# Cross-attention and maxout layers on one core: PSUM pools regrouped, three weight products run as one group, a subtraction moved to GpSimd

## The chip, the cores and the metric

The kernel runs on one core of one Trainium2 chip. Times are device microseconds (us) of whole executions; each number given for a kernel is the median of several, with the lowest and highest. One execution of each kernel was also profiled, and the times inside a kernel are read from that trace. The span in a profile is some 1.8 us shorter than the time of the same execution. PE is TensorE, DVE is VectorE, ACT is ScalarE, POOL is GpSimd, SPq is the queue of the engine that issues transfers.

## The reference, cut to what matters

```python
# attention between x (8 batches, 8 heads, 512 tokens, 64) and a state of 32 rows per head
a  = softmax(scale * x @ state.T)      # 512 x 32 per head
xread = a @ state
a2 = softmax(scale * state @ x.T)
sread = a2 @ x
t  = concat([xread, sread])            # per batch 544 rows of 512
# maxout layer on all 4352 rows
out = maximum(t @ w1, t @ w2) @ w_out  # w1, w2: 512 x 1024; w_out: 1024 x 512
```

The kernel uses max(h1, h2) = max(h1 - h2, 0) + h2. With Wc = [W1 - W2, W2 Wout], 512 x 1536, and a the attention weights, it forms S Wc once per batch (S is the state, so this is small), then a (S Wc): the first 1024 columns go through a relu and Wout, the other 512 are added to the output. So each batch needs: scores, exp, normalisation, `a` transposed into `aT`, S Wc in three chunks of 512 columns, a first layer (aT times S Wc, 16 matmuls of 512 columns), and four output chunks of 10 matmuls each.

## The kernel before

PSUM is used as two pools of four banks, one for the output chunks (`acc`), one for everything else (`ps`):

```python
psum = ctx.enter_context(tc.tile_pool(name="ps", bufs=4, space=bass.MemoryType.PSUM))
accs = ctx.enter_context(tc.tile_pool(name="acc", bufs=4, space=bass.MemoryType.PSUM))
```

A chunk of S Wc takes two banks, eight matmuls of 64x32 tiles, and two copies out. For the batches below TWO the first two chunks are computed as S W1 - S W2, in two terms, since W1 - W2 (`wcat`) isn't there yet:

```python
def u_sw(b, ch, engs="VA"):
    pg = [bank(), bank()]
    two = b < TWO and ch < 2               # TWO = 3
    terms = ((sbd, w1b), (sneg, w2b)) if two else ((sbd, wcat),)
    ...                                    # 8 matmuls per term
    for g in range(2):
        copy(engs[g], SW[b][:, g, ch * 512:(ch + 1) * 512], pg[g])
```

The attention of batch n = b + 1 is woven between the output chunks of batch b. Slot 8 stands behind output chunk 0, slot 11 behind chunk 3:

```python
put(8, lambda: u_sc(n, 0), lambda: u_sc(n, 1))          # scores, exp, normalisation
put(8, lambda: compact_x(n + 1, 0), lambda: compact_x(n + 1, 1))
put(9, lambda: u_sw(n, 0))
put(10, lambda: u_sw(n, 1), lambda: u_sr(n))
put(10, lambda: d_at(n))                                # transposing DMA: aT <- a
put(10, lambda: d_xt(n + 1))                            # transposing DMA: xt <- xc, right behind it
put(11, lambda: u_srt(n), lambda: u_sw(n, 2))
```

And in the loop over batches, on VectorE:

```python
if b == 1:
    put_states(rest, sT)                   # copy of the states of batches 3..7 into sbd
    fill[9].append(lambda: w_sub(0))       # W1 - W2, a quarter each, on VectorE
    fill[11].append(lambda: w_sub(1))
if b == 2:
    fill[8].append(lambda: w_sub(2))
    fill[9].append(lambda: w_sub(3))
```

The softmax here doesn't subtract the row's maximum and nothing guards it: scores larger than these inputs give would overflow.

## Time and profile before

| | before |
|---|---|
| time, us | 159.56 (158.77 to 160.09, 3 runs) |
| span of the profiled execution | 158.4 |
| mean granted TensorE clock in it | 0.984 |

The chain of waits is the work that ended last, followed back from the last instruction. I cut it into stages at the start of each batch's first layer and at the scores:

| stage of the chain, us | before |
|---|---|
| 1 until batch 1's first layer begins | 43.90 |
| 2 that layer | 4.41 |
| 3 first layers of batches 2 to 7 | 21.94 |
| 4 from the scores to the next first layer, six times | 53.69 |
| output chunk 0, ahead of the scores, six times | 12.96 |
| 5 from the end of the last first layer to the end | 21.49 |
| sum | 158.39 |

### The profile page before, as it was taken

The page shows a single profiled execution, that of the slowest core. Times are in us where ns is not written, and L with a number is a line of the kernel's source. Part 1 is how long each engine was busy: PE and PEld are TensorE (multiplying, and loading weights), DVE is VectorE, ACT ScalarE, POOL GpSimd, SP SyncE. Part 2 cuts the span into 40 slices and gives each one's busy share as a digit, 9 for nine tenths or more (in the row PEclk, how much of TensorE's full clock was granted, in tenths as well). Part 3 has the DMA queues.
Part 4 walks back from the last instruction along what each step waited for, and adds up shares of the span by engine and source line. Part 5 has one row for each costly group of instructions (what it writes and reads, how often), then busy time and mean ns, then how long its engine had stood idle before and what let it go on. Part 6 is the DMA issues. An engine that isn't in the chain of part 4 may idle for free.

```text
span 158.4 us, 3054 instructions
## 1 busy us (share of the span) xinstructions
PE 145.6 (92%) x1272; PEld 67.4 (43%) x1272; DVE 92.2 (58%) x155; ACT 74.5 (47%) x125; POOL 35.1 (22%) x40
## 2 busy tenths in 40 slices
PE   6779699997789999988999999999999999999990
PEld 1356353343435334523453444445444534664430
DVE  5378367946995849595755466555647554731110
ACT  3064357635773828452746447363827234621100
POOL 3015300800740540074005402520500050000000
PEclk9978999999999999999999999999999999999998
DMA  3999999669499299909981997593079033501531
GB/s 92 371 390 389 384 377 290 232 116 227 152 289 291 73 106 326 302 0 105 345 284 25 152 299 256 38 297 132 0 107 342 19 35 82 217 0 37 163 137 66
DMA packets 37789, 29.88 MB, mean 189 GB/s; under 512 B 24848, under 2 KB 33040, under 8 KB 36880
## 3 DMA queue, kind: packets, MB, share of 16 engines
q1 hardware_dynamic: 37776, 29.69, 68.5%
q8 instruction: 10, 0.16, 0.5%
q14 instruction: 3, 0.02, 0.1%
HBM read 15.20 MB, written 8.91 MB: 152 GB/s over the span
## 4 chain that ended last, share of the span: by engine, by line
PE 72%; DVE 10%; DMA 10%; ACT 2%; POOL 2%; issue 1%; SPq 0%; DVEq 0%; POOLq 0%; ACTq 0%
PE acc L315 27%; PE ps L300 16%; PE acc L311 7%; PE acc L387 4%; PE ps L275 4%; DMA xf<-in_x_dram 4%; DMA aT<-a 3%; DMA xt<-xc 3%; PE ps L213 2%; PE ps L342 2%; PE acc L352 2%; POOL a L223 2%; PE ps L376 2%; PE ps L236 1%; DVE es L220 1%; DVE sbd L64 1%
## 5 line engine op out<-in xcount | busy, mean ns | idle before, releaser
L315 PE MATMUL acc<-wo,r 128*128 128x512 bf16 x256 | 60.8, 379 | 0.0
L315 PEld LDWEIGHTS <-r 128*128 128x128 bf16 x256 | 24.7, 98 | 29.9 <-issue 0.8
L300 PE MATMUL ps<-aT,swt 128*128 128x512 bf16 x128 | 29.9, 379 | 0.9 <-DVE r L290 0.4
L223 POOL TENSOR_TENSOR a<-e,er 128x512 bf16<-128x512 bf16 x13 | 14.4, 1124 | 63.0 <-ACT e L216 38.3
L290 DVE TENSOR_SCALAR r<-ps 128x512 bf16<-128x512 f32 x32 | 21.8, 690 | 7.9 <-PE ps L300 7.6
L64 DVE COPY ob<-acc 128x512 f32<-128x512 f32 x16 | 11.0, 686 | 23.0 <-PE acc L315 23.0
L288 ACT ACTIVATE r<-ps 128x512 bf16<-128x512 f32 x32 | 19.3, 602 | 8.9 <-PE ps L300 8.8
L64 DVE CAST swt<-ps 128x512 bf16<-128x512 f32 x24 | 16.4, 685 | 12.0 <-PE ps L275 12.0
L62 ACT CAST swt<-ps 128x512 bf16<-128x512 f32 x24 | 14.3, 595 | 14.0 <-PE ps L275 14.0
L62 ACT COPY ob<-acc 128x512 f32<-128x512 f32 x16 | 9.4, 590 | 21.2 <-PE acc L315 19.9
L300 PEld LDWEIGHTS <-swt 128*128 128x128 bf16 x128 | 11.8, 97 | 16.9 <-issue 2.7
L311 PE MATMUL acc<-swt,aT 128*128 128x512 bf16 x64 | 18.7, 381 | 0.0
L66 POOL CAST xp<-xf 128x2048 bf16<-128x2048 f32 (+1 forms) x8 | 14.1, 1762 | 14.3 <-DMA xf<-in_x_dram 14.3
L216 ACT ACTIVATE e<-ps 128x512 bf16<-128x512 f32 x16 | 8.8, 595 | 14.9 <-PE ps L213 14.9
L62 ACT CAST xc<-xf 128x1024 bf16<-128x1024 f32 x13 | 13.0, 1051 | 0.0
L220 DVE TENSOR_REDUCE es<-e 128x16 f32<-128x512 bf16 x16 | 10.6, 662 | 2.5 <-ACT e L216 2.5
L133 PE MATMUL ps<-warm 128*128 128x512 bf16 x18 | 7.2, 541 | 1.3 <-POOL warm L119 1.3
L275 PE MATMUL ps<-wcat,sbd 64*32 64x512 bf16 x144 | 7.4, 387 | 1.1 <-DVE wcat L361 1.1
L387 PE MATMUL acc<-wo,w2t 128*128 128x512 bf16 x32 | 7.4, 379 | 0.0
L311 PEld LDWEIGHTS <-aT 128*128 128x128 bf16 x64 | 4.9, 97 | 5.4 <-issue 1.8
L275 PEld LDWEIGHTS <-sbd 64*32 64x32 bf16 x192 | 2.7, 89 | 10.4 <-issue 8.4
L213 PE MATMUL ps<-sbd,xt 128*128 128x64 bf16 x128 | 5.4, 196 | 1.5 <-DMA xt<-xc 0.8
(65 smaller groups left out, 109.2 us busy)
## 6 DMA issues: line engine op xcount, KB each, us to landing
xf<-in_x_dram SPq DMA_DIRECT2D x8, 1024.0 KB, 7.7
out_dram<-ob SPq DMA_DIRECT2D x7, 1024.0 KB, 5.1
w2f<-in_moe_w_dram SPq DMA_DIRECT2D x2, 1024.0 KB, 10.1
wof<-in_moe_w_out_dram SPq DMA_DIRECT2D x4, 512.0 KB, 11.4
w1f<-in_moe_w_dram SPq DMA_DIRECT2D x2, 1024.0 KB, 15.3
out_dram<-ob SPq DMA_DIRECT2D x4, 256.0 KB, 2.0
out_dram<-obs SPq DMA_DIRECT2D x8, 64.0 KB, 1.7
s_f<-in_state_dram SPq DMA_DIRECT2D x1, 320.0 KB, 13.8
```

Source lines behind the costliest of these rows:

```text
L62: nc.scalar.copy(o, i)
L64: nc.vector.tensor_copy(o, i)
L66: nc.gpsimd.tensor_copy(o, i)
L220: nc.vector.tensor_reduce(d["es"][:, g], d["e"][:, g].rearrange("p i c n -> p (i c) n"), axis=mybir.AxisListType.X, op=ALU.add)
L223: mul.tensor_mul(d["a"][:, g].rearrange("p c i n -> p i c n"), d["e"][:, g], d["er"][:, g].rearrange("p (i c) -> p i c", i=4).unsqueeze(3) ...
L275: nc.tensor.matmul(pg[g][32 * i:32 * i + 32, :], sneg[gs, b, i, :] if k else sbd[gs, b, 2 * i + g, g, :], w[gs, i, ch * 512:(ch + 1) * 512 ...
L288: nc.scalar.activation(out=o, in_=p, func=ACTF.Relu)
L290: nc.vector.tensor_scalar(o, p, scalar1=0.0, scalar2=None, op0=ALU.max)
L300: nc.tensor.matmul(p, SW[b][:, g, f * 128:(f + 1) * 128], AT[b][:, g, :], start=(g == 0), stop=(g == 1))
L311: nc.tensor.matmul(OB[b][1 + c], AT[b][:, g, c * 128:(c + 1) * 128], SW[b][:, g, FF:WC], start=(g == 0), stop=False)
L315: nc.tensor.matmul(OB[b][1 + c], R[b][:, f, c * 128:(c + 1) * 128], wo[:, f, :], start=False, stop=(f == NF - 1))
L387: nc.tensor.matmul(WO[i], w2t[:, i, f, :], wo[:, f, :], start=(f == 0), stop=(f == NF - 1))
```

## The change

Its intent is to take waits and small costs from around TensorE, which is busy 92% of the time. It has five parts: the start is put in another order (the w2b cast earlier, both halves of x1 on ScalarE, one warm-up of three matmuls fewer); PSUM is one ring of eight banks once batch 1 begins; the three S Wc chunks of a batch run as one group; W1 - W2 goes to GpSimd and is ready before batch 2 (batch 1 uses its first half, in one of its two chunks); the last output chunk is computed and stored in halves. The copy of the late states moves from the beginning to the end of batch 1.

```diff
-    TWO = 3
+    TWO = 2
+    def one_ring():
+        early.close()                     # the two pools of 4
+        pools["ps"] = pools["acc"] = ctx.enter_context(tc.tile_pool(name="ring", bufs=8, ...))
-    def u_sw(b, ch, engs="VA"):
+    def sw_mm(b, ch, engs="VA"):          # matmuls now, copies later
...
-        two = b < TWO and ch < 2
+        two = b < TWO and ch < 2 and (b, ch) != (1, 0)
...
+        return lambda: [copy(engs[g], SW[b][:, g, ch * 512:(ch + 1) * 512], pg[g]) for g in range(2)]
+    def u_sw(b, *chs):
+        for out_of in [sw_mm(b, ch) for ch in chs]:
+            out_of()
...
-            put(9, lambda: u_sw(n, 0))
-            put(10, lambda: u_sw(n, 1), lambda: u_sr(n))
-            put(10, lambda: d_at(n))
+            put(9, lambda: u_sr(n))
+            put(10, lambda: u_sw(n, 0, 1, 2), lambda: d_at(n))
...
-            put(11, lambda: u_srt(n), lambda: u_sw(n, 2))
+            put(11, lambda: u_srt(n))
...
-        nc.vector.tensor_sub(wcat[:, :, cs], w1f[:, :, cs], w2f[:, :, cs])
+        nc.gpsimd.tensor_sub(wcat[:, :, cs], w1f[:, :, cs], w2f[:, :, cs])
...
     w_cast(w1b, w1f, 0)                   # at the start
+    w_sub(0)
+    w_sub(1)
...
         if b == 1:
-            put_states(rest, sT)
-            fill[9].append(lambda: w_sub(0))
-            fill[11].append(lambda: w_sub(1))
-        if b == 2:
-            fill[8].append(lambda: w_sub(2))
-            fill[9].append(lambda: w_sub(3))
+            fill[11].append(lambda: put_states(rest, sT))
```

Cut here: the new order of the start, `l2_end` (two halves of 256 columns, each with its copy and its store, on two queues), and a helper.

More of the change, by code (lines that the diff above doesn't have):

```diff
@@ L49, with bank @@
     big = ctx.enter_context(tc.tile_pool(name="big", bufs=2))
-    psum = ctx.enter_context(tc.tile_pool(name="ps", bufs=4, space=bass.MemoryType.PSUM))
-    accs = ctx.enter_context(tc.tile_pool(name="acc", bufs=4, space=bass.MemoryType.PSUM))
+    early = ctx.enter_context(ExitStack())
+    pools = dict(ps=early.enter_context(tc.tile_pool(name="ps", bufs=4, space=bass.MemoryType.PSUM)),
+                 acc=early.enter_context(tc.tile_pool(name="acc", bufs=4, space=bass.MemoryType.PSUM)))
     ctx.enter_context(tc.manual_schedule())
-    def bank(dtype=F32):
-        return psum.tile([128, 512 if dtype == F32 else 1024], dtype, tag="ps", name="ps")
+    def bank(dtype=F32, kind="ps"):
+        return pools[kind].tile([128, 512 if dtype == F32 else 1024], dtype, tag="b", name=kind)
     def acc():
-        return accs.tile([128, 512], F32, tag="acc", name="acc")
+        return bank(kind="acc")
+    def one_ring():
+        early.close()
+        pools["ps"] = pools["acc"] = ctx.enter_context(tc.tile_pool(name="ring", bufs=8, space=bass.MemoryType.PSUM))
     def copy(eng, o, i):
@@ L68, in negate @@
     def negate(eng, o, i):
-        if eng == "A":
-            nc.scalar.activation(out=o, in_=i, func=ACTF.Copy, scale=-1.0)
-        else:
-            (nc.vector if eng == "V" else nc.gpsimd).tensor_scalar(o, i, scalar1=-1.0, scalar2=None, op0=ALU.mult)
+        (nc.vector if eng == "V" else nc.gpsimd).tensor_scalar(o, i, scalar1=-1.0, scalar2=None, op0=ALU.mult)
     def run(*units):
@@ L170, with new_x @@
     st = {}
+    def new_x(b):
+        if b not in st:
+            st[b] = dict(xt=at.tile([128, 2 * H, 128], BF16, tag="xt", name="xt"))
     def cast_x(b, parts=(("P", slice(0, 8)),)):
-        xp = xio.tile([128, H, NC, 66], BF16, tag="xp", name="xp")
+        new_x(b)
+        xp = st[b]["xp"] = xio.tile([128, H, NC, 66], BF16, tag="xp", name="xp")
         nc.gpsimd.memset(xp[:, :, :, 64:65], 1.0)
@@ L177, in cast_x @@
             copy(e, xp[:, hs, :, 0:64], xf_t[b][:, hs].rearrange("p h (c d) -> p h c d", c=NC))
-        st[b] = dict(xp=xp, xt=at.tile([128, 2 * H, 128], BF16, tag="xt", name="xt"))
     def compact_x(b, g, eng="A"):
+        new_x(b)
         if g == 0:
@@ L278, in u_sw @@
                                      start=(k == 0), stop=(k == len(terms) - 1))
-        for g in range(2):
-            copy(engs[g], SW[b][:, g, ch * 512:(ch + 1) * 512], pg[g])
+        return lambda: [copy(engs[g], SW[b][:, g, ch * 512:(ch + 1) * 512], pg[g]) for g in range(2)]
+    def u_sw(b, *chs):
+        for out_of in [sw_mm(b, ch) for ch in chs]:
+            out_of()
     flip = [0]
@@ L327, in l2 @@
     def l2(b, fill):
-        for c in range(NC):
+        for c in range(NC - (b == B - 1)):
             l2_open(b, c)
@@ L334, in l2, with l2_end @@
             l2_out(b)
+        else:
+            l2_end(b, NC - 1)
+    def l2_end(b, c):
+        ob = OB[b][0]
+        dst = out[b * L:b * L + S].rearrange("(p c) n -> p c n", c=NC)
+        cs = slice(c * 128, (c + 1) * 128)
+        for h in range(2):
+            hs = slice(h * 256, (h + 1) * 256)
+            p = acc()[:, 0:256]
+            mm = [(AT[b][:, g, cs], SW[b][:, g, FF + h * 256:FF + (h + 1) * 256]) for g in range(2)]
+            mm += [(R[b][:, f, cs], wo[:, f, hs]) for f in range(NF)]
+            for k, (w, v) in enumerate(mm):
+                nc.tensor.matmul(p, w, v, start=(k == 0), stop=(k == NF + 1))
+            copy("A" if h else "V", ob[:, c, hs], p)
+            (nc.scalar if h else nc.sync).dma_start(out=dst[:, c:c + 1, hs], in_=ob[:, c:c + 1, hs])
     def moe_sread():
@@ L432 @@
     u_norm(0, 1, nc.vector)
+    negate_states()
     warm_up(3)
-    for i in range(4):
-        w_wo(0, i)
-    for i in range(4):
-        w_wo(1, i)
+    for q in range(2):
+        for i in range(4):
+            w_wo(q, i)
+    w_cast(w2b, w2f, 1)
+    wo_cast(2, "P")
+    w_t(1, 0, "V")
+    w_t(1, 1, "A")
     u_at(0, "V")
     u_srt(0)
-    w_cast(w2b, w2f, 1)
-    negate_states()
-    w_t(1, 0, "V")
-    w_t(1, 1, "A")
-    wo_cast(2, "P")
     wo_cast(3, "V")
-    warm_up(3)
     for i in range(4):
@@ L449 @@
     w_cast(w1b, w1f, 0)
-    w_wo(3, 0)
-    w_wo(3, 1)
+    w_sub(0)
+    w_sub(1)
+    for i in range(4):
+        w_wo(3, i)
     u_sw(0, 0)
-    w_wo(3, 2)
-    w_wo(3, 3)
-    l1(0, {}, range(0, 2))
     u_sw(0, 2)
-    l1(0, {}, range(2, 4))
-    cast_x(1)
+    l1(0, {}, range(0, 4))
     for c in range(NC):
@@ L461 @@
     w_cast(w1b, w1f, 1)
-    compact_x(1, 0, "A")
-    compact_x(1, 1, "V")
+    compact_x(1, 0)
+    compact_x(1, 1)
     d_xt(1)
+    cast_x(1)
+    w_sub(2)
+    w_sub(3)
     cast_states("P", rest)
+    load_x(3)
     sT = d_states(rest)
@@ L474 @@
     cast_x(2)
-    load_x(3)
     l2_add(0, 0, range(4, 8))
@@ L480 @@
     l2_close(0, 1)
+    u_sw(1, 1)
+    u_sr(1)
     compact_x(2, 0)
     compact_x(2, 1)
-    u_sw(1, 1)
-    u_sr(1)
-    u_at(1, "V")
     l2_add(0, 2, range(4, 8))
     l2_close(0, 2)
-    u_sw(1, 2)
-    u_srt(1)
+    u_at(1, "V")
     l2_add(0, 3, range(4, 8))
@@ L492 @@
     d_xt(2)
+    u_sw(1, 2)
+    u_srt(1)
     l2_out(0)
+    one_ring()
     for b in range(1, B):
```

## The prediction

> **What bounds the kernel now.** I read the page's busy shares first, then the chain that ended last, then TensorE's own waits, then the timeline around each wait.
>
> ```profile
> PE 145.6 (92%) x1272; PEld 67.4 (43%) x1272; DVE 92.2 (58%) x155; ACT 74.5 (47%) x125; POOL 35.1 (22%) x40
> ...
> PE 72%; DVE 10%; DMA 10%; ACT 2%; POOL 2%; issue 1%; SPq 0%; DVEq 0%; POOLq 0%; ACTq 0%
> ```
>
> TensorE (PE) is busy 92% of the span and makes 72% of the chain. So a gain must come from fewer matmuls on TensorE or from its few waits. VectorE (DVE) and transfers have 10% of the chain each, some 16 us each. TensorE's waits with a named cause are short:
>
> ```profile
> PE ps L376 <- DVE w2b L64: 1.5, 1, 1.5
> ...
> PE ps L275 <- DVE wcat L361: 1.1, 1, 1.1
> PE ps L254 <- DVE swt L64: 0.9, 1, 0.9
> PE ps L213 <- DMA xt<-xc: 0.8, 1, 0.8
> ...
> PE ps L300 <- DVE r L290: 0.4, 1, 0.4
> PE ps L300 <- DMA aT<-a: 0.3, 1, 0.3
> ```
>
> All of these are waits that the change touches. The chain in order of time shows one steady batch (start us, us, what):
>
> ```profile
> 95.70 0.47 PE ps L213 x16
> 96.17 0.43 PE acc L311 x2
> 96.60 1.73 PE acc L315 x8
> 98.32 0.34 PE ps L275 x8
> 98.66 0.54 PE acc L311 x2
> 99.20 1.73 PE acc L315 x8
> 100.93 0.34 PE ps L275 x8
> 101.27 0.37 PE ps L236 x30
> 101.64 0.54 PE acc L311 x2
> 102.17 1.73 PE acc L315 x8
> 103.90 0.06 PE ps L260
> 103.96 0.34 PE ps L275 x8
> 104.30 3.69 PE ps L300 x16
> ```
>
> TensorE has no hole here: scores (L213), output chunks of 2.16 (L311 and L315), three S Wc chunks (L275) of 0.34 each, then the next batch's first layer (L300) of 3.6 to 3.7. From scores to that layer is 8.60, and a whole batch 14.4. But the attention goes another way at the same time: scores, exp, sums, the product on GpSimd (POOL), a transposing DMA into aT, and only then L300. In batch 2 this is what ended last:
>
> ```profile
> 68.14 1.52 DVE L361 TENSOR_TENSOR wcat<-w1f,w2f 128x1024 bf16<-128x1024 f32 x1
> ...
> 70.59 1.24 SPq L245 DMA_TRANSPOSE aT<-a  x1
> ...
> 71.70 0.41 PE L275 MATMUL ps<-wcat,sbd 64*32 64x512 bf16 x8 [1.09 <-DVE wcat L361]
> ...
> 75.47 2.76 PE L300 MATMUL ps<-aT,swt 128*128 128x512 bf16 x12 [0.33 <-DMA aT<-a]
> ```
>
> The subtraction on VectorE holds TensorE 1.09 us, and aT lands at 75.42, just ahead of L300. The trace's landings of aT, against the start of L300: 59.55 and 59.60, 75.42 and 75.47, 89.86 and 89.93, 104.11 and 104.30, 118.11 and 118.74, 132.30 and 133.18. The first four batches have no slack there; this decides what the regrouping is worth.
>
> [...]
> - [...] this cast takes 0.69 us elsewhere and 1.70 here, ending about 0.55 after GpSimd's does.
>
> ```profile
> 27.96 1.89 POOL L66 CAST xp<-xf 128x2048 bf16<-128x2048 f32 x1 [8.61 <-DMA xf<-in_x_dram]
> ...
> 28.70 1.70 DVE L64 CAST w1b<-w1f 128x1024 bf16<-128x1024 f32 x1
> ```
>
> - [...] No such operation is in this trace; its bf16 product of 512 elements takes 1.05, which scales to 2.1.
> - [...] eight 64x32 matmuls take 0.34, sixteen take 0.56, so eight more cost 0.22 and each entry some 0.12; the 128x128 pair after them takes 0.54 instead of 0.43.
>
> **The change part by part.** Stages are cut by the chain of waits.
>
> 1. Until batch 1's first layer begins (43.90 before). The w2b cast moves ahead of the aT copy on VectorE. Its data landed at 15.72 by the trace, so the transposes (L376) can follow the matmuls that end at 17.95; the 1.5 us hole goes, and so does a warm-up of 0.65. All four w_wo(3) chunks then end near 23.0. Now the w1 columns bound: they land at 22.15, ScalarE's cast takes 1.05, so S W1 starts near 23.3 (24.26 before); the first layer's four pieces must wait for the WO copies and swt copies, near 25.1, and end near 26.9 (28.07 before): 1.2 us earlier. Next the x1 data land at 27.91 whatever I do; both compact halves are now on ScalarE, 2 x 1.05, so the transposing DMA starts near 30.1 (32.13 before[...]), and at 4.4 lands near 34.6. I allow 0.4 for load_x(3), now issued beside it. Scores near 34.9 (36.59 before). Then VectorE's in-order copies, 7.3 us before, set the rest: batch 1 begins near 42.3. Saved 1.6. The subtractions[...] end before the product that needs GpSimd at about 38.5.
> 2. Batch 1's first layer, 43.90 to 48.31, 4.41. VectorE copied sbd from sT in it for 1.93, the four PSUM banks filled and TensorE stopped. That copy goes to the end of batch 1, and the ring has 8 banks. A free run is about 3.65. Saved 0.75. (The copy then delays VectorE's relus in batch 2 by some 1 us; 8 banks take that up.)
> 3. First layers of batches 2 to 7, six times 3.63 to 3.69. With no swt copy in front of the relus and 8 banks I put them at 3.55 (sixteen times 0.216 is 3.46). Saved 0.6.
> 4. From scores to the next first layer, six times: 9.13, 10.09, 8.67, 8.60, 8.60, 8.60. TensorE's own work becomes 0.47 + 3 x 2.16 + 2 x 0.11 + 0.37 + 0.06 + SW (0.12 + 3 x 0.22 = 0.78) = 8.38, 0.22 under the 8.60; the two-term S W of batch 2 falls to the same. But aT doesn't get faster: it landed 9.08, 10.04, 8.60, 8.41, 7.97, 7.72 after the scores. Only the second changes: without the subtraction the aT issue is 4.2 after the scores, as in the others, not 5.2, so 9.0. The later of the two gives 9.1, 9.05, 8.65, 8.45, 8.38, 8.38 = 52.0, against 53.7. Saved 1.7, of which 1.05 is the subtraction and only 0.65 the group.
> 5. The end. The last copy of 512 columns on ScalarE takes 0.59, and its store of 256 KB lands 2.06 later. A half has 256 columns, 0.38 by the rs rows, and 128 KB; the 64 KB stores land in 1.7. Saved 0.2 + 0.2 = 0.4. The halved matmuls cost nothing: N = 256 runs at 0.109 each (32 in 3.49).
>
> Sum 1.6 + 0.75 + 0.6 + 1.7 + 0.4 = 5.05. From 159.56 that is 154.5; I add 0.2 for small frictions of a new order and say **154.7**.
>
> **The rivals.**
> - The regrouping gives its whole 0.22 per batch and aT follows. For: aT lands later where the xt transpose is issued close behind it (4.97 and 4.83) than in batch 6, which has none (3.50), so another order of transfers could speed it. Against: the same two transfers stay in the same order. TensorE's 8.38 six times is 50.3, 1.7 us under my 52.0: 153.0.
> - The subtraction on GpSimd takes the place of VectorE's: [...] cast_states and the product of batch 1 slip. For: both engines are woken by the same landing. Against: at 7.61 VectorE started 0.03 ahead of GpSimd on such a landing. Stage 1 would lose 1.3: 156.0.
> - load_x(3), issued early, slows the xt transpose by more than my 0.4, up to 2 us. For: 1 MB behind it in the same queues. It would cost 1 to 1.5: about 156.
> - Six banks taken at once make TensorE wait for copies. Against: when the group is issued, its banks' last users (two relus, one output chunk, two scores, another chunk) ended over 2 us earlier. It would cost 0.3 a batch, 156.5.
>
> **Range and chances.** The certain parts are the subtraction in batch 2 (1.05), the sbd copy (0.75) and the end (0.4); with those alone it is 157.4. The start is a chain of many orders, and two rivals bear on it. If it gives nothing, 156.3; if all rivals for the better hold, 153. A range of 153.0 to 156.6 should hold 8 of 10. Faster by over 2% means under 156.4: 0.86. Within 2%: 0.13. Slower: 0.01.
>
> **What would show it.** Step 1: scores of batch 1 near 35, the first layer of batch 1 near 42.3, and no wait of L376 for w2b. Step 2: 3.65 for that layer and no wait for a relu. Step 4: in batches 1 to 3 TensorE's wait for aT grows from 0.3 in total to 1.2 to 1.6; no wait for the subtraction; S Wc as one group of 0.78. If that wait stays small, and the interval is 8.4 in batches 1 to 3 too, the first rival is right. VectorE's busy time falls by 5.5[...]. If GpSimd's subtractions take 3 us or more each, or the w1b cast on VectorE is over 2 us, the second rival is right; if the first xt transpose takes over 5.5, the third. Wrong altogether if a wait for PSUM banks appears before L275 in each batch.

## More of the kernel before

The clock is one more thing to look at before two traces are compared. This row of the page gives the granted clock in 40 slices of the span, 9 for full speed. Before:

```profile
PEclk9978999999999999999999999999999999999998
```

There was one dip, in the third and fourth slice; the trace's clock records put it at 10.01 to 13.42 us.

## The result, and the profile after

The changed kernel took 155.44 us at the median of 4 runs (152.12 to 158.12); the kernel before, beside it, 159.6. The ratio of fast runs is 0.9589, with a 95% interval of 0.9476 to 0.9703: faster. A ratio is the mean time of one kernel's fast runs over that of the other's of the same rounds, so not quite the ratio of the medians. Here the difference matters: an execution more than 1.5% above the fastest of its kernel is labelled slow and left out, and the changed kernel spreads over 6 us, so the ratio rests on the two fastest of its four runs. The medians give 155.44 / 159.6 = 0.974.

The spread is itself a finding. The kernel before lies within 158.5 and 160.7 in all its runs here. The changed kernel's ten executions took 152.12, 152.56, 153.81, 154.25, 154.86, 155.56, 155.84, 156.88, 157.06 and 158.12.

The profiled execution took 153.81, with a span of 152.0. The page's busy shares and the chain's shares:

```profile
PE 142.4 (94%) x1255; PEld 68.7 (45%) x1255; DVE 85.5 (56%) x151; ACT 75.4 (50%) x126; POOL 44.4 (29%) x44
...
PE 84%; DVE 7%; DMA 4%; ACT 2%; issue 0%; SPq 0%
```

The chain is now 84% TensorE, from 72%; VectorE's part falls from 10 to 7 and that of transfers from 10 to 4. TensorE does 17 matmuls fewer, VectorE loses 6.7 us, GpSimd gains 9.3. The chain, stage by stage, against the prediction and against the quietest variant (experiment plus16 below):

| stage of the chain, us | before | predicted | changed | plus16 |
|---|---|---|---|---|
| 1 until batch 1's first layer | 43.90 | 42.3 | 43.86 | 42.24 |
| 2 that layer | 4.41 | 3.65 | 3.62 | 3.62 |
| 3 six first layers | 21.94 | 21.3 | 20.70 | 20.70 |
| 4 scores to first layer, six | 53.69 | 52.0 | 50.10 | 50.10 |
| output chunk 0, six | 12.96 | - | 12.96 | 12.96 |
| 5 the end | 21.49 | 21.1 | 20.80 | 20.8 |
| sum | 158.39 | | 152.04 | 150.4 |

So stage 1 gave nothing in this execution, where 1.6 was expected, and stages 3 and 4 gave 4.83, where 2.3 was expected. The sum came out near the number all the same. A steady batch of the changed kernel in the chain (start us, us, what):

```profile
77.56 0.47 PE ps L221 x16
...
80.19 0.37 PE ps L244 x32
80.55 0.54 PE acc L322 x2
...
82.82 0.77 PE ps L283 x24
83.59 0.54 PE acc L322 x2
84.13 1.73 PE acc L326 x8
85.85 0.06 PE ps L268
85.91 3.45 PE ps L311 x16
```

L221 is the scores, L283 the S Wc, L311 the first layer (L213, L275 and L300 before). The group of 24 takes 0.77 where three groups of 8 took 0.34 each. The first layer comes 8.35 after the scores, where it was 8.60, and takes 3.45, where it was 3.69: what stands just in front of it is now an ordinary 128x128 transpose (L268) and no longer a group of 64x32 matmuls. There is no aT anywhere in this chain, and among TensorE's waits none for aT.

**Stage 1.** The clock row of this execution:

```profile
PEclk9965999999999999999999999999999999999999
```

The dip is longer: the records show half the clock for 6.83 us (8.97 to 15.80), where the profile of before has it for 3.41. TensorE came to the first WO matmul at 15.88 instead of 14.33, and everything behind it on VectorE was late too. The timeline of GpSimd and of VectorE (start us, us, engine, line, what):

```profile
21.73 5.41 POOL L389 TENSOR_TENSOR wcat<-w1f,w2f 128x1024 bf16<-128x1024 f32 x2 [2.82 <-DMA w1f<-in_moe_w_dram]
```

```profile
22.08 2.85 DVE L70 CAST w1b<-w1f 128x1024 bf16<-128x1024 f32 x1
```

The w1 columns landed at 21.65. VectorE was still in its w_out cast, GpSimd began 0.35 us ahead of it, and VectorE's w1b cast needed 2.85 us instead of 0.69, ending 0.55 after GpSimd's first subtraction (24.92 and 24.37). That is the prediction's second rival, come true in this execution. The kernel before shows the like twice: casts of the same form that began while GpSimd was in a cast took 1.70 and 1.74 us, and each ended 0.55 after it. What holds VectorE there the traces don't show. It turns on which of the two begins first, so on tenths of a microsecond; the next profile shows the other outcome. Dip and long cast can be told apart by the profile of sub_back below: it has as long a dip (8.41 to 15.24, first WO matmul at 15.73) and no subtraction on GpSimd, its cast took 0.69, and its batch 1 began at 42.72. So most of the 1.4 us between this execution's 43.86 and the next profile's 42.42 goes with the long cast.

### The profile page after: what moved, and what is told of

Same layout as the page of the kernel before. It is cut to its first block, busy times and chain, and to the rows that moved or that the text cites.

```text
span 152.0 us, 3031 instructions
## 1 busy us (share of the span) xinstructions
PE 142.4 (94%) x1255; PEld 68.7 (45%) x1255; DVE 85.5 (56%) x151; ACT 75.4 (50%) x126; POOL 44.4 (29%) x44
## 4 chain that ended last, share of the span: by engine, by line
PE 84%; DVE 7%; DMA 4%; ACT 2%; issue 0%; SPq 0%
PE acc L326 34%; PE ps L311 18%; PE acc L322 10%; DMA xf<-in_x_dram 4%; PE ps L283 3%; PE ps L221 2%; PE ps L370 2%; PE acc L380 2%; PE acc L415 2%; DVE w1b L70 2%; PE ps L244 2%; PE ps L404 2%; PE acc L360 1%; PE ps L203 1%; PE acc L378 1%; PE ps L136 1%
## 5 line engine op out<-in xcount | busy, mean ns | idle before, releaser
L326 PE MATMUL acc<-wo,r 128*128 128x512 bf16 x248 | 58.9, 379 | 0.0
L326 PEld LDWEIGHTS <-r 128*128 128x128 bf16 x248 | 23.9, 98 | 28.8 <-issue 0.6
L231 POOL TENSOR_TENSOR a<-e,er 128x512 bf16<-128x512 bf16 x13 | 13.4, 1048 | 63.1 <-ACT e L224 29.9
L311 PE MATMUL ps<-aT,swt 128*128 128x512 bf16 x128 | 29.1, 379 | 1.0 <-ACT sread_t L68 0.8
L70 DVE COPY ob<-acc 128x512 f32<-128x512 f32 (+1 forms) x17 | 11.4, 671 | 27.4 <-PE acc L326 27.0
L68 ACT CAST swt<-ps 128x512 bf16<-128x512 f32 x24 | 12.9, 592 | 14.2 <-PE ps L283 14.2
L311 PEld LDWEIGHTS <-swt 128*128 128x128 bf16 x128 | 12.1, 98 | 15.4 <-DVE swt L70 1.5
L68 ACT COPY ob<-acc 128x512 f32<-128x512 f32 (+1 forms) x16 | 9.2, 576 | 15.9 <-PE acc L326 10.9
L70 DVE CAST swt<-ps 128x512 bf16<-128x512 f32 x24 | 15.2, 679 | 1.9 <-PE ps L283 1.9
L68 ACT CAST xc<-xf 128x1024 bf16<-128x1024 f32 x14 | 13.9, 1051 | 0.0
L389 POOL TENSOR_TENSOR wcat<-w1f,w2f 128x1024 bf16<-128x1024 f32 x4 | 10.6, 2660 | 2.8 <-DMA w1f<-in_moe_w_dram 2.8
L283 PE MATMUL ps<-wcat,sbd 64*32 64x512 bf16 x168 | 6.8, 380 | 0.2 <-DVE wcat L70 0.2
L221 PEld LDWEIGHTS <-xt 128*128 128x128 bf16 x128 | 5.0, 102 | 2.8 <-ACT xt L68 0.7
```

Source lines behind the costliest of these rows:

```text
L68: nc.scalar.copy(o, i)
L70: nc.vector.tensor_copy(o, i)
L231: mul.tensor_mul(d["a"][:, g].rearrange("p c i n -> p i c n"), d["e"][:, g], d["er"][:, g].rearrange("p (i c) -> p i c", i=4).unsqueeze(3) ...
L283: nc.tensor.matmul(pg[g][32 * i:32 * i + 32, :], sneg[gs, b, i, :] if k else sbd[gs, b, 2 * i + g, g, :], w[gs, i, ch * 512:(ch + 1) * 512 ...
L311: nc.tensor.matmul(p, SW[b][:, g, f * 128:(f + 1) * 128], AT[b][:, g, :], start=(g == 0), stop=(g == 1))
L326: nc.tensor.matmul(OB[b][1 + c], R[b][:, f, c * 128:(c + 1) * 128], wo[:, f, :], start=False, stop=(f == NF - 1))
```

## The experiments

Each kernel was correct, and was timed beside the kernel before on the same chip; "the fetch" in what follows is explained under the second. Unless a diff says otherwise, the edit is made to the changed kernel. The times from the issue of aT's transfer to its landing are given for batches 2 to 7 in order.

### again: the changed kernel unaltered

No edit.

> The changed kernel once more, unaltered. Its first four times were 152.1, 153.8, 157.1 and 158.1 us, so it has two groups 4 us apart, which the granted clock doesn't explain (1.0, 0.978, 0.989, 0.976). Theory A (the transposing DMA into aT meets the fetch of TensorE's instructions in some executions): a slow execution has aT landings of 4.2 to 5 us after issue as the kernel before had, a fast one 3.2 in batches 1 to 4. Theory B (the chip or the time of day): all times of this call lie in one group. If the profile is a fast one: first layer of batch 1 near 43.9, scores to next first layer 8.35.

Measured: 155.21 us (152.56 to 156.88, 6 runs), ratio 0.9625 (0.955 to 0.970). In its profile, again of VectorE and GpSimd:

```profile
21.88 0.69 DVE L70 CAST w1b<-w1f 128x1024 bf16<-128x1024 f32 x1 [1.90 <-DMA w1f<-in_moe_w_dram]
```

```profile
21.93 5.17 POOL L389 TENSOR_TENSOR wcat<-w1f,w2f 128x1024 bf16<-128x1024 f32 x2 [3.05 <-DMA w1f<-in_moe_w_dram]
```

VectorE was 0.05 us ahead of GpSimd, its cast took 0.69, and batch 1's first layer began at 42.42, where the prediction said 42.3 and this run's expectation 43.9. The six times don't lie in one group, so theory B is out. GpSimd's pair took 5.17. So did the second pair of the first profile, where the two can be read one by one: the first, begun 0.05 after a VectorE cast of 0.68, took 2.86, the second, with no such cast beside it, 2.34.

But this execution took 154.25, a little more than the first one, and not for its start. Theory A fits it: its aT transfers took 3.27, 3.26, 3.32, 5.07, 4.47 and 3.55 us, and after the two long ones the scores-to-layer interval was 9.59 and 8.98 (from the first matmul of one to the first of the other) instead of 8.35. In the first profile of the changed kernel the six took 3.27, 3.22, 3.28, 3.20, 3.79 and 3.51.

### wo3_pool: VectorE free when the w1 columns land

```diff
-    wo_cast(3, "V")
+    wo_cast(3, "P")
```

> One letter changed: the last cast of w_out goes from VectorE to GpSimd, so VectorE is idle when the w1 columns land. [...] VectorE's cast of w1 then starts first and takes 0.7 us instead of 2.85, GpSimd's first subtraction waits for it; S W1 begins 1 us earlier against the landing of w1, and batch 1's first layer 0.5 to 1 us earlier. Rival (the landing of x1 bounds the start): the cast is fast but batch 1 begins when it did, and the time is the same within 0.3.

Measured: 155.96, 152.16, 152.21 and 154.74; ratio 0.9549 (0.9487 to 0.9611). VectorE's cast took 0.69, but it did so in again as well, without the edit. Batch 1 began at 41.81, only 0.6 before again's 42.42. So this run doesn't tell the theories of stage 1 apart. What it does show is the other thing. Its profiled execution, the one of 155.96, waits for aT four times. TensorE's waits, then one of them in the timeline:

```profile
PE ps L311 <- DMA aT<-a: 3.6, 4, 1.1
```

```profile
56.42 1.89 PE L311 MATMUL ps<-aT,swt 128*128 128x512 bf16 x8 [0.49 <-DMA aT<-a]
```

aT took 4.60, 4.97, 4.98, 5.09, 3.55 and 3.11; the intervals were 9.00, 9.49, 9.50, 9.61, 8.35 and 8.35. aT is issued 4.38 after the scores (4.26 in batch 2), and where the first layer waits for it, it begins 0.14 after the landing. So a transfer up to 8.35 - 4.38 - 0.14 = 3.8 is hidden, and beyond that each microsecond is paid. Note that the profile is labelled slow, at a clock of 0.997; the clock isn't what makes it slow, and the argument does not rest on it alone.

The view of the transfers, cut from the issue of aT to its landing, shows what is in the long ones. The row GB/s has 40 slices of the stretch; then come the queues (packets, MB, share of 16 engines' time). First this kernel, batch 2:

```profile
GB/s 0 0 0 0 0 0 0 0 0 0 91 214 223 211 218 223 200 211 191 176 134 134 274 209 218 216 194 122 38 24 11 7 9 9 9 11 9 9 185 289
...
q8 instruction: 1, 0.02, 1.3%
```

Then the kernel before, the transfer issued at 70.59 that the prediction shows, 4.83 us long:

```profile
GB/s 0 0 0 0 0 0 0 0 0 17 167 224 220 218 212 207 214 201 169 123 113 163 351 214 209 195 118 21 8 0 0 0 6 8 11 8 11 8 28 277
...
q8 instruction: 1, 0.02, 1.5%
```

And the changed kernel's first profile, batch 2, 3.3 us from issue to landing:

```profile
GB/s 0 0 0 0 0 0 0 0 0 0 0 0 0 0 50 169 219 232 232 213 213 210 225 191 210 207 197 175 132 132 141 116 207 216 244 185 235 194 232 194
...
q1 hardware_dynamic: 1619, 0.41, 65.7%
```

A slice is 0.115, 0.121 and 0.082 us. In the third the rate stays between 116 and 244 GB/s until aT has landed. In the other two it holds for some 18 slices, falls to about 10 GB/s for ten to twelve slices (1.2 and 1.5 us), and then aT lands. Only these two have a packet of the queue called "instruction". It is one packet of 16,384 bytes, and its spacing fits TensorE: ten such packets for 2510 matmuls and weight loads (the page counts 1255 of each), and in the steady batches of this run 258 to 262 of them from one packet to the next, though 195 to 264 over the whole trace. So I take it for the fetch of TensorE's next instructions. That is my reading; what the packet holds the trace doesn't say. But with sixteen TensorE instructions more at the start these packets began within half a microsecond of the issue of aT in all six batches (plus16), where the first profile of the changed kernel has 5.2 us or more in four of them. No wait of TensorE is put down to its instructions, but the landing of a transposing DMA in flight is late by up to 1.9 us (5.1 against 3.2).

A steady batch has 129 matmuls and as many weight loads, so 258 instructions, nearly the distance of two packets here (258 to 262). The fetch therefore falls on almost the same place of several batches in a row. In this run its packets began 2.6 to 3.1 us after the issue of aT, between the packets of the aT and the xt transposes; in the first profile of the changed kernel 5.2 to 5.35 after it in batches 2 to 5, behind both. This gives a theory to test: the changed kernel stands on an edge, and where the fetch falls decides up to 1.26 us per batch (9.61 against 8.35). It also puts a question to my prediction, which took the late aT of the kernel before for a property of the two transfers.

### plus16: sixteen TensorE instructions more

```diff
     warm_up(5)
+    pt = bank()
+    for k in range(8):
+        nc.tensor.matmul(pt[:, 0:1], warm[:, 0:128], warm[:, 0:1], start=(k == 0), stop=(k == 7))
```

Eight matmuls of one column, 0.34 us, in a hole in which TensorE waits for x0 anyway. They compute nothing that is used; they only shift the fetches by 16 instructions.

> Eight matmuls of one column (16 TensorE instructions) added in the hole before x0 lands, where they cost nothing. A steady batch has 258 TensorE instructions [...] the fetch comes at nearly the same place in each batch, and 16 instructions move it to before the transposes of aT. Fetch theory: no fetch inside any of the six aT transposes; all six land 3.2 to 3.3 us after issue (in the changed kernel the last two took 3.8 and 3.5), and the slow group of times is gone or its share changes. Rival (the transposes' time has nothing to do with fetches): landings and times as in the changed kernel.

Measured: 152.21, 152.02, 151.95, 152.07; median 152.05, ratio 0.9538 (0.9488 to 0.9588). The spread of 6 us is gone in these four runs, and in the eight of states_back16 and end_whole16 below, which have the same 16 instructions. Every aT took 3.04 to 3.29, every interval 8.35, and the fetches began between 0.26 before and 0.44 after the issue, ahead of the first packets of aT, which come 1.1 after it:

```profile
DMA to landing us min/median/max: 3.0/3.2/3.3
```

One of these four ran at a clock of 0.977, and was the fastest, so the clock doesn't order these times. This is the best version that was quiet in all its runs: it beats both kernels.

### no_group: the S Wc chunks back in their old slots

```diff
-            put(9, lambda: u_sr(n))
-            put(10, lambda: u_sw(n, 0, 1, 2), lambda: d_at(n))
+            put(9, lambda: u_sw(n, 0))
+            put(10, lambda: u_sw(n, 1), lambda: u_sr(n))
+            put(10, lambda: d_at(n))
...
-            put(11, lambda: u_srt(n))
+            put(11, lambda: u_srt(n), lambda: u_sw(n, 2))
```

> The three S Wc chunks go back to their old slots in each batch; the ring of 8 banks and all else stays. Group theory: TensorE's own work from scores to the next first layer is 8.57 to 8.60 instead of 8.35, and the first layer 3.6 instead of 3.45 because the last swt copies stand ahead of the relus: 0.35 a batch, 2.1 us in all. Rival (what gained is that aT no longer meets the fetch): if the fetch moves back into aT, the interval is 8.6 to 9.1 with TensorE waiting for aT, and the loss is over 3 us; if not, aT lands at 3.2 and TensorE doesn't wait.

Measured: 157.08, 157.0, 156.54, 157.28; ratio 0.9849 (0.9804 to 0.9895). That is 5.0 above plus16, over the 3 that the rival named. And aT took 4.71, 4.91, 4.79, 4.77, 4.94 and 3.05, with intervals of 9.02, 9.34, 9.21, 9.20, 9.36 and 8.69: moving the matmuls had moved the place of the fetch as well (2.5 to 2.9 after the issue). So this run mixes two effects, and no_group86 below is needed to part them.

Its last transfer is a control that came by itself. Batch 7 has the fetch at the same place, 2.47 after the issue, but no xt transpose behind it, since there is no batch 8. aT landed after 3.05:

```profile
GB/s 0 0 0 0 0 0 0 0 0 0 0 0 0 0 0 44 161 218 225 225 215 228 198 228 188 218 208 201 218 188 198 189 283 20 0 0 0 0 0 0
...
q8 instruction: 1, 0.02, 2.9%
```

Batch 7 of no_group16 below shows the same (2.51, 3.05). So in these runs a fetch at this place made aT late only where a second transpose followed (3.05 in these two, 4.6 to 5.1 in the 17 transfers with one).

### minus8: fewer instructions

```diff
-    warm_up(1)
...
-    warm_up(3)
```

Four matmuls, eight instructions, taken away.

> The changed kernel with 8 TensorE instructions fewer ahead of the steady batches (four warm-up matmuls left out, in a wait for a copy). The fetch is asked for 8 instructions later in each batch, some 0.9 us. Fetch theory: it now always comes among the packets of the aT transpose, as in the kernel before: aT lands 4.4 to 5.1 us after issue in at least four batches, scores to the next first layer take 9.0 to 9.6 there, and all times lie in one slow group, 156 to 157.5. Rival (adding any small matmul early helps by itself, by warming or by moving the start): times as the changed kernel's, spread from 152 to 158, or worse only by a lost warm-up.

Measured: 151.87, 152.05, 151.66, 158.25. I had expected a late aT in all of them, and three of four are quiet: a miss. In the profiled one every aT took 3.05 to 3.33, and the fetches began 5.2 to 5.5 after the issue in batches 2 to 6 (4.1 in batch 7), behind both transposes: where the first profile of the changed kernel had them (5.2 to 5.35), although eight instructions were gone. The fourth run was not profiled; its 158.25 is at the level of the changed kernel's worst. The two profiles of the changed kernel show that the place is not fixed by the code: in batch 5 the fetch began 5.35 after the issue in one and 3.03 in the other. What decides it in one execution stays open.

### before32: the kernel before, with its fetches moved

```diff
     warm_up(5)
+    pt = bank()
+    for k in range(16):
+        nc.tensor.matmul(pt[:, 0:1], warm[:, 0:128], warm[:, 0:1], start=(k == 0), stop=(k == 15))
```

> The kernel before with 16 one-column matmuls (32 instructions) in the hole ahead of x0. Fetch theory: the fetch leaves aT in most batches, which lands 3.1 to 3.4 us after issue instead of 3.5 to 5.0. But TensorE's own work there was 8.57 to 8.60 against 9.13, 10.09, 8.67 and 8.60 measured, so little is won: 0.3 to 0.9 us, 158.6 to 159.2. That is, before the regrouping the late aT was nearly hidden. Rival (the fetches cost the kernel before as much as the changed one): 156 to 157.

Measured: 159.66, 159.84, 158.47, 158.43, beside 160.21 for the kernel before; ratio 0.9951 (0.9886 to 1.0015). All six transfers became short:

```profile
DMA to landing us min/median/max: 3.0/3.3/3.3
```

Unaltered, they took 4.98, 4.83, 4.39, 4.19, 3.75 and 3.50. So the late aT of the kernel before was not the two transfers alone: with xt as close behind (1.3 to 1.8 after aT) and no fetch in the way they are short. It cost little there: the intervals, from matmul to matmul, went from 9.29, 10.25, 8.82, 8.70, 8.69, 8.69 to 9.12, 9.85, 8.69 four times, 0.7 in sum, since TensorE's own work took 8.69 anyway, and the first two had the two-term S W and the subtraction besides.

### no_group16 and no_group86: the old slots, with the fetches moved by 16 and by 86 instructions

```diff
     # no_group, and ahead of cast_x(0):
+    pt = bank()
+    for k in range(8):                    # no_group86: range(43)
+        nc.tensor.matmul(pt[:, 0:1], warm[:, 0:128], warm[:, 0:1], start=(k == 0), stop=(k == 7))
```

> The chunks of S Wc in their old slots, with the 8 small matmuls of the quiet version, to price the grouping where no fetch disturbs. aT should land 3.1 to 3.4 after issue. Group theory: scores to the next first layer 8.57 to 8.69 (8.35 with the group), first layer to scores 5.61 to 5.75, so 1.3 to 2.2 us in all above the quiet version's 152.05: 153.4 to 154.3. Rival (the group's worth in the changed kernel was only the place of the fetch): within 0.5 us of 152.05.

> The ungrouped kernel with 43 one-column matmuls (86 instructions) instead of 8. With 16 instructions its fetches still came 2.5 to 3.1 us after the aT issue, between the packets of aT and xt, aT took 4.7 to 5.0, and it ran 156.9. Fetch theory: 86 instructions bring the fetch ahead of the aT issue, aT lands 3.0 to 3.4 after issue in all batches, scores to the next first layer take 8.57 to 8.69 instead of 9.2 to 9.5, and the time falls to 153.4 to 154.3. This one change of place is then worth 2.5 to 3.5 us, and the grouping itself 1.3 to 2.2 over the quiet grouped kernel (152.05). Rival (the group is what makes aT fast): the time stays at 156.5 to 157.3.

Measured: no_group16 157.25, 156.28, 157.25, 156.49, median 156.87, ratio 0.9808 (0.9753 to 0.9863). A miss: 16 instructions were too few, the fetch stayed among the packets. no_group86 154.52, 154.34, 154.35, 154.43, median 154.39, ratio 0.967 (0.9625 to 0.9716), just above the range expected. The two differ by 35 matmuls of one column at the start, and the one with more work is 2.5 us faster; all eight runs are fast ones. They were timed on different chips, on which the kernel before took 160.21 and 159.61 at the median; by the ratios the difference is 2.2. It is not from the start: batch 1 begins at 42.23 in no_group16 and at 42.43 in no_group86. The transfers of no_group16:

```profile
DMA to landing us min/median/max: 3.0/4.9/5.0
```

of no_group86:

```profile
DMA to landing us min/median/max: 3.0/3.0/3.3
```

And one transfer of each as above, no_group16 first:

```profile
GB/s 0 0 0 0 0 0 0 0 0 75 215 223 217 207 217 213 201 176 128 118 163 335 205 205 187 114 28 0 0 0 0 0 6 6 10 8 10 10 36 274
...
q8 instruction: 1, 0.02, 1.8%
```

```profile
GB/s 0 0 0 0 0 0 0 0 0 0 0 0 0 0 0 37 148 219 205 219 192 232 202 189 94 54 219 280 266 273 280 253 68 21 0 0 0 0 0 24
```

With the fetch out of the way the rate holds until aT's packets are through, and only the last 0.4 us before the landing are empty. The six intervals fall from 9.16, 9.47, 9.17, 9.34, 9.29, 8.69 (55.12) to 8.69 six times (52.14), 2.98 less, for 2.48 of the time. This is the run that shows what the fetch's place costs without any change to the batches. It also prices the grouping on quiet ground: 154.39 against 152.05 of plus16 and 152.08 of states_back16, the latter on the same chip, so 2.3 us. Six times 8.69 - 8.35 = 0.34 makes 2.04 of it; most of the rest is the start (42.43 against 42.03), where no_group86 has 35 matmuls more.

### sub_back: W1 - W2 on VectorE again

```diff
-    TWO = 2
+    TWO = 3
...
-        two = b < TWO and ch < 2 and (b, ch) != (1, 0)
+        two = b < TWO and ch < 2
...
-        nc.gpsimd.tensor_sub(wcat[:, :, cs], w1f[:, :, cs], w2f[:, :, cs])
+        nc.vector.tensor_sub(wcat[:, :, cs], w1f[:, :, cs], w2f[:, :, cs])
```

with the four `w_sub` calls back in their old slots.

> The subtraction goes back to VectorE, to its old places in batches 1 and 2, and S W of the first three batches back to two terms; all else is as changed. By count the fetch should be 48 instructions earlier and quiet. Theory of step 4: two-term chunks cost 0.22 each (one in the start, two in batch 1), and in batch 2 TensorE waits about 1 us for the subtraction: 1.5 to 2 us above the quiet 152.05, that is 153.5 to 154.1. Rival (with 8 banks and the late group the subtraction is hidden): under 0.8 us.

Measured: 154.44, 154.0, 153.67, 154.17, median 154.08; ratio 0.9628 (0.9571 to 0.9686). Its intervals are 8.78, 9.27 and 8.35 four times, its first aT took 3.89 and the others 3.0 to 3.3. Against the three quiet runs of minus8 on the same chip (151.66 to 152.05) the subtraction's move is worth about 2.2, with the two-term products that it spares; its two late intervals show 0.43 + 0.92 = 1.35 of it, and 0.80 is the start (batch 1 at 42.72 against 41.92), which had a longer clock dip in this profile.

### no_ring86: no_group86 without the one ring

```diff
-    one_ring()
```

> The same with two pools of 4 banks to the end instead of the ring of 8. Theory: in the steady batches 4 banks were enough (the kernel before had no bank wait there), so the ring by itself is worth under 0.5 us; only in batch 2, where the sbd copy stands ahead of the relus, can the first layer stall, by up to 1 us. Expect 0.3 to 1.2 us more than the ungrouped quiet kernel. Rival (the ring is what shortens the first layer from 5.75 to 5.61 in every batch): 0.8 us spread over six batches.

Measured: 154.57 (154.34 to 154.73) beside 154.39. In five batches the scores begin 5.75 after the first layer instead of 5.62, which is 0.65 in sum; in the chain those first layers take 3.68 instead of 3.56. But this execution's batch 1 began 0.66 earlier (41.77 against 42.43), so the difference of the times, 0.18, decides nothing: the ring's gain is seen in the chain, not in the time. The expected 0.3 to 1.2 was missed, and the rival's 0.8 over six batches is near the chain's 0.65. Batch 1's first layer took 3.62, so the copy of the states does no harm at its new place with two pools either.

### states_back16: plus16 with the copy of the states at its old place

```diff
-            fill[11].append(lambda: put_states(rest, sT))
+            put_states(rest, sT)
```

> The quiet version with the sbd copy back at the start of batch 1. Theory of step 2: the copy of 1.9 us stands ahead of VectorE's relus in batch 1; with 4 banks TensorE stopped 0.75 us. With 8 banks the first layer runs through, but the first output chunks then wait for late relus of r: 0.2 to 0.8 us more, 152.2 to 152.9. Rival (the ring alone takes it up): within 0.15 us of 152.05.

Measured: 152.0, 152.16, 152.0, 152.38, median 152.08: the same as plus16, as the rival said. Batch 1's first layer took 3.62 here too. With no_ring86 this means: either the ring or the copy's new place is enough to take away the stall; both together give nothing more.

### end_whole16: plus16 with the last chunk whole

```diff
-        for c in range(NC - (b == B - 1)):
+        for c in range(NC):
...
-        else:
-            l2_end(b, NC - 1)
```

> The quiet version (8 small matmuls) with the last 128 rows as one chunk, one copy and one store, as before. Theory of step 5: the tail after the last matmul is 0.4 to 0.9 us longer (4.57 before and 3.73 in the changed kernel, from the start of the last matmul to the end): 152.5 to 152.9. Rival (the second queue costs what the halves win): 151.9 to 152.3.

Measured: 152.57, 152.09, 152.47, 152.31, median 152.39, against 152.08 of states_back16 on the same chip: the halves are worth about 0.3, between the two expectations. From the start of the last matmul to the end it is 4.16, against 3.75 in plus16: 0.41.

## Why the prediction was right or wrong

The number was right: 155.44 measured at the median for 154.7 predicted, inside 153.0 to 156.6, and faster as it said. Its steps were less so, and two errors stood against each other: in the profiled execution the start gave 1.6 too little and the steady batches 2.5 too much. That they cancelled is luck.

- **Step 1, the start: right in mechanism and size, but not in each execution.** Predicted start of batch 1: 42.3. The other profiles of the changed kernel and its variants show 41.77 to 42.43, and sub_back's 42.72. The first one shows 43.86, since a longer clock dip made VectorE late, and GpSimd began a third of a microsecond ahead. The rival had estimated the loss at 1.3; it was 1.6, of which the clock dip has a small part (sub_back). My argument against that rival (VectorE starts 0.03 ahead on such a landing) holds only where both engines are waiting; nothing in the kernel keeps VectorE idle at that time. That the subtraction fits on GpSimd before its product is needed was right: four of 2.34 to 2.86 us in the first profile, where the prediction had scaled GpSimd's bf16 product to 2.1, the last ending at 34.53, and the product began at 40.01.
- **Step 2, batch 1's first layer: right.** 3.65 predicted, 3.62 measured. The reason was half of it: I named both the copy's move and the ring. Either alone does it (states_back16, no_ring86).
- **Step 3, the six first layers: mechanism right, size off.** I put a layer at 3.55; it took 3.45, so 1.24 in all instead of 0.6. The experiments divide the 0.24 that a layer lost: 3.69 before and 3.68 with two pools (no_ring86), 3.56 with the ring and the third chunk still in front of the layer (no_group86), 3.45 with the group. So the ring gives 0.12 or 0.13, which makes my 3.55, and the other 0.11 goes with the third chunk in front of the layer. I put it down to the change from 64x32 to 128x128 matmuls, since a pair of output matmuls behind such a group loses as much (0.54 for 0.43); that is an estimate, as no run parts it from the copies of that chunk. I had priced this change between the S Wc groups and the output chunks and missed it here.
- **Step 4, from scores to layer: the step that failed.** TensorE's own work was right: 8.38 predicted, 8.35 measured. I then set the later of that and of aT, and let aT land as late as before, 9.1, 9.05, 8.65 and 8.45 after the scores in the first four batches, because "the same two transfers stay in the same order". That sentence is the error. Without a fetch of instructions in the way the same transfers in the same order are 3.0 to 3.4 us long (before32); with it they were 4.2 to 5.0. So in a quiet execution all six intervals are 8.35, and the step gives 3.6 instead of 1.7: the first rival's result. The rival named the xt transpose close behind as the cause and had half of it: a fetch between the two made aT late only where xt followed (no_group, batch 7). Its sign, the one transfer without xt (3.50; "batch 6" there, since the prediction counts by the loop), had the fetch elsewhere (0.74 after the issue). In an execution with the fetch among the packets it gives nothing: wo3_pool's intervals sum to 54.3, where before they are 54.4 from matmul to matmul. The test I had set, that TensorE's wait for aT would grow to 1.2 to 1.6 in batches 1 to 3, came out at no wait at all in one profile, 1.5 us in again and 3.6 in wo3_pool. My number lies between two states, and is near the median of the kernel because its executions are spread over both.
- **Step 5, the end: right.** 0.4 predicted, 0.41 between end_whole16 and plus16. From before to after the chain lost 0.69; the rest of that is not explained.
- **The other rivals.** The first xt transpose took 4.4 to 5.0 in all profiles, where over 5.5 was the rival's sign, and no wait for PSUM banks stands before the group. VectorE lost 6.7 us where 5.5 was predicted, and GpSimd gained 9.3.

What each part is worth, on quiet ground: the subtraction about 2.2, the grouping 2.0 to 2.3, the halves 0.3, the ring some 0.7 in the chain (six layers of 0.12) but not clear in the time, the copy's new place nothing once the ring is there. The new order of the start was not undone by itself; the chain's 43.90 to 42.24 is all that there is on it.

What was shown and what was only argued: that a few idle instructions of TensorE move the time by 2.2 to 2.5 us is shown (no_group16 against no_group86). So is what goes with it, over the 84 aT transfers of the 14 profiles:

| a fetch begins, us after the issue of aT | xt transpose behind | transfers | aT took, us |
|---|---|---|---|
| 2.5 to 3.1 | yes | 17 | 4.6 to 5.1 |
| 2.5 | no | 2 | 3.05 |
| 0.5 to 1.5 | 8 of 10 | 10 | 3.5 to 4.5 |
| none from 0.5 to 3.1 | either | 55 | 3.0 to 3.55 |

In a transfer of the first row it need not be the moving of aT's data that is late. In wo3_pool's batch 2 the 32 packets of 4 bytes that end each aT transfer begin 2.36 to 2.71 after the issue, in the quiet batch 2 of the first profile 2.37 to 2.72; but the landing comes at 4.60 instead of 3.27. Why the rate falls to 10 GB/s and the landing waits is not visible in the trace. And why the fetch goes in between the two transposes in one execution and behind both in another, for the same program, stays open; so does a way to guarantee its place other than to count instructions and measure.

## What to carry to other kernels

When a transfer takes longer than another of the same form and size, look at what shares its stretch of time before calling the lateness its own; here the queue view cut to one transfer named a culprit that no wait names, and the two transfers with no neighbour showed that it doesn't act alone. When the packets of the instruction queue come about once in each turn of a kernel's loop (here 258 TensorE instructions a batch, and 258 to 262 from packet to packet in the steady batches of wo3_pool), they fall on nearly the same spot in turn after turn, so a change that only adds or moves instructions can gain or lose by that, here up to 2.5 us of 157: compare variants at more than one offset before crediting the change. And where VectorE and GpSimd wake on one landing, don't let the order of arrival decide: VectorE's cast took 0.69 us where it began 0.05 ahead and 2.85 where it began 0.35 behind, and both came in executions of the same kernel here.
